# The order of the first loads of a pruned matrix product: a token pair ahead of the weights, on the other DMA queue

## The chip, the cores and the metric

The kernel runs on one core of one Trainium2 chip. The metric is the time of one execution on the device in microseconds (us), lower is better. The kernel before took 232.98 us (median of 3 runs, 232.91 to 233.33).

## The reference

A dense layer whose weight matrix is pruned on the fly. `x` is 16 x 512 x 1024 (8192 tokens of 1024 values), `w` is 1024 x 1024 and `b` has 1024 values, all in bf16. Down each column of `w` the rows form groups of four, and a weight is kept where its magnitude is at least the second largest of its group.

```python
wg = w.reshape(G, M, D)                       # G = 256, M = 4
mag = jnp.abs(wg)
order = jnp.argsort(mag, 1)
thr = jnp.take_along_axis(mag, order[:, M - N:M - N + 1, :], 1)   # N = 2
mask = mag >= thr
wp = (wg * mask).reshape(D, D)
return jnp.einsum("bsd,df->bsf", x, wp) + b
```

## The kernel before

The 8192 tokens are 64 tiles of 128. The product of a tile needs the tokens transposed (the 1024 input values on the partitions, in 8 blocks of 128) and the pruned weights. Two output halves `h` of 512 columns each fill one PSUM bank per tile.

Most tiles (14 to 63) are plain: their tokens come in through transposing DMAs, and 16 matmuls of 512 columns, one behind another, make a tile (L369); VectorE adds the bias and writes the output tile (L248). This part begins when all weights are pruned and takes about three quarters of the time.

Before that the weights have to be loaded and pruned, and TensorE should have work meanwhile. This is the front, whose order is written out by hand in the string `FRONT` (L285 to L299). One token of the string is one step, and each engine does its share of the steps in the string's order:

- `W` and `w`: a matmul on constants, 512 and 128 columns wide, whose result nobody reads (`warm`, L105). They fill TensorE's time at the start.
- `T.t`: tile t's first 512 input values are transposed by TensorE in four matmuls against an identity (L182); it waits for the tile's load. `C.t`: ScalarE copies them from PSUM (L187).
- `A.i` and `P.i`: VectorE takes the magnitudes of weight piece i (L120), then per group of four rows: `hi`, the larger of rows 0, 1 and of rows 2, 3 (L133); `lo`, the smaller of each (L134); `t1`, the smaller of the two `hi` (L137); `t2`, the larger of the two `lo` (L141); `thr`, the larger of `t1` and `t2` (L143); then the mask (L150) and the pruned weights (L153), for rows 0 and 1 first and rows 2 and 3 after them. On partition p of the weight tile lie the four rows of one group, so rows 0, 1 and rows 2, 3 are two halves of each partition. The threshold needs both halves.
- `N.i.t.m`: the matmuls of weight piece i with tile t for the rows m alone (L203); `M.i.t` is all four rows. Piece 0 is columns 0 to 255 of the first 512 input rows (its matmuls have 256 columns).

Piece 0 is the first that is needed. It comes in as two transfers of 128 KB, rows 0, 1 and rows 2, 3 (`load_w`, L71). Tokens 0 to 7 (their first 512 values) come in pairs or singly (`load_x`, L79): tiles 0 and 1 in one transfer of 256 KB, 2 and 3 in one, 4 and 5 singly with 128 KB each, 6 and 7 in one. Two DMA queues are used, that of the sync engine SP and that of ScalarE (ACT). Each queue does its transfers in order. ScalarE issues its transfers before it loads its function table and makes its first copy (L100).

The order of the first loads, by queue:

| queue | 1st | 2nd | 3rd | 4th | 5th | 6th |
|---|---|---|---|---|---|---|
| SP | piece 0 rows 0, 1 | tiles 0, 1 | tile 4 | tile 5 | piece 1 | tiles 6, 7 |
| ACT | piece 0 rows 2, 3 | tiles 2, 3 | | | | |

Then come larger transfers on SP: the second column half of the first 512 weight rows, another weight piece, and from L259 the transposed tokens of tiles 8 to 13.

Of the kernel before, what the change touches and what calls it, by code (L numbers as in the profile page):

```python
# [10 lines left out]
def kernel(  # L11
# [7 lines left out]
    nc = tc.nc  # L19
    P = 128  # L20
    bf16 = mybir.dt.bfloat16
    fp32 = mybir.dt.float32
    u16 = mybir.dt.uint16
    Alu = mybir.AluOpType
    Act = mybir.ActivationFunctionType
    K = tc.keep_in_program_order

    B, S, D = x.shape
# [10 lines left out]
    T, F = 8, 6  # L39
# [25 lines left out]
    def w_of(i):  # L65
        g, c0, c1 = pieces[i]
        return w_gh[(g, c0 // FH)][:, :, c0 % FH:c0 % FH + c1 - c0]

    def load_w(g, c0, c1, eng=nc.sync, m0=0, m1=4):
        dst = w_gh[(g, c0 // FH)][:, m0:m1, c0 % FH:c0 % FH + c1 - c0]  # L70
        K(eng.dma_start(dst, wv[:, g, m0:m1, c0:c1]))  # L71
# [4 lines left out]
    def load_x(ta, tb, eng=nc.sync):  # L76
        xt = const.tile([P, tb - ta, KH], bf16, name=f"xh_{ta}")
        src = xf[ta * P:tb * P, 0:KH].rearrange("(t p) c -> p t c", p=P)
        K(eng.dma_start(xt[:], src))  # L79
        for t in range(ta, tb):  # L80
            xh[t] = xt[:, t - ta, :]

    load_w(0, 0, 256, nc.sync, 0, 2)
    load_w(0, 0, 256, nc.scalar, 2, 4)
    load_x(0, 2)
    load_x(2, 4, nc.scalar)
    load_x(4, 5)
    load_x(5, 6)
    load_w(0, 256, 512)
    load_x(6, 8)  # L90
    load_w(0, 512, 1024)
# [14 lines left out]

    mags = {}

    def abs_piece(i, on_act):
        g, c0, c1 = pieces[i]  # L110
        n = c1 - c0
        if n <= 256:
            mag = mags_pool.tile([P, 4, n], bf16, name="mag")[:]
        else:
            mag = mag2_pool.tile([P, 4, n], bf16, name="mag2")[:]
        if on_act:
            K(nc.scalar.activation(mag, w_of(i), Act.Abs))
        else:
            for ms in (slice(0, 2), slice(2, 4)) if i == 0 else (slice(0, 4),):
                K(nc.vector.tensor_single_scalar(  # L120
                    mag[:, ms].bitcast(u16), w_of(i)[:, ms].bitcast(u16), 0x7FFF, op=Alu.bitwise_and))
        mags[i] = mag

    def prep_piece(i):
        g, c0, c1 = pieces[i]
        n = c1 - c0
        mag = mags.pop(i)
        magv = mag.rearrange("p (a j) f -> p a j f", j=2)
        hi = tmp.tile([P, 2, FH], bf16, name="hi")[:, :, :n]
        lo = tmp.tile([P, 2, FH], bf16, name="lo")[:, :, :n]  # L130
        for a in ((0, 1), (1, 2)) if i == 0 else ((0, 2),):
            a = slice(*a)
            K(nc.vector.tensor_tensor(hi[:, a], magv[:, a, 0, :], magv[:, a, 1, :], op=Alu.max))  # L133
        K(nc.vector.tensor_tensor(lo, magv[:, :, 0, :], magv[:, :, 1, :], op=Alu.min))  # L134
        t1 = tmp.tile([P, FH], bf16, name="t1")[:, :n]
        t2 = tmp.tile([P, FH], bf16, name="t2")[:, :n]
        K(nc.vector.tensor_tensor(t1, hi[:, 0, :], hi[:, 1, :], op=Alu.min))  # L137
        thr = tmp.tile([P, FH], bf16, name="thr")[:, :n]
        cols = (slice(0, n // 2), slice(n // 2, n)) if i == 0 else (slice(0, n),)
        for c in cols:  # L140
            K(nc.vector.tensor_tensor(t2[:, c], lo[:, 0, c], lo[:, 1, c], op=Alu.max))  # L141
        for c in cols:
            K(nc.vector.tensor_tensor(thr[:, c], t1[:, c], t2[:, c], op=Alu.max))  # L143
        mask = tmp.tile([P, 4, FH], bf16, name="mask")[:, :, :n]

        halves = (slice(0, 2), slice(2, 4)) if i < 3 else (slice(0, 4),)

        def keep(ms, c=slice(0, n)):
            tb = thr[:, None, c].to_broadcast([P, ms.stop - ms.start, c.stop - c.start])
            K(nc.vector.tensor_tensor(mask[:, ms, c], mag[:, ms, c], tb, op=Alu.is_ge))  # L150

        def prune(ms, c=slice(0, n)):
            K(nc.vector.tensor_tensor(w_of(i)[:, ms, c], w_of(i)[:, ms, c], mask[:, ms, c], op=Alu.mult))  # L153

        if i == 0:
            for step in (keep, prune):
                for c in cols:
                    step(halves[0], c)
            keep(halves[1])
            prune(halves[1])  # L160
        else:
            for ms in halves:
                keep(ms)
            for ms in halves:
                prune(ms)
# [100 lines left out]
    def issue_batch(t0, nb):  # L266
# [16 lines left out]


    FRONT = """  # L285
        I.1.0.512 D.0 A.0 P.0 W W W W W W W W W w w T.0 T.1 C.0 T.2 T.3 C.1 w T.4 C.2 N.0.0.0 N.0.0.1 T.5
        N.0.1.0 N.0.1.1 N.0.0.2 N.0.0.3 N.0.1.2 N.0.1.3 M.0.2 A.1 C.3 P.1 U.0.0.0.512 I.1.512.1024 G C.4 C.5
        M.0.3 N.0.4.0.1 T.6 T.7 C.6 N.0.4.2.3 C.7 A.2 M.0.5 M.0.6 P.2 M.0.7 N.1.0.0.1 N.1.1.0.1 A.3
        N.1.2.0.1 N.1.0.2.3 N.1.1.2.3 N.1.2.2.3 V.0.0 M.1.3 V.0.1 M.1.4 V.0.2 M.1.5 M.1.6 V.0.3 M.1.7 V.0.4
        P.3 N.2.0.0.1 V.0.5 N.2.1.0.1 N.2.0.2.3 V.0.6 N.2.1.2.3 M.2.2 V.0.7 M.2.3 M.2.4 M.2.5 M.2.6 A.4 P.4  # L290
# [9 lines left out]
    for tok in FRONT.split():  # L300
# [6 lines left out]
        elif k in "Ww":  # L307
            warm(FH if k == "W" else P)
        elif k == "A":
            abs_piece(n[0], n[0] == 3)  # L310
        elif k == "P":
            prep_piece(n[0])
        elif k == "T":
            transpose_half(n[0])
# [89 lines left out]
```

## Time and profile before

| what | value |
|---|---|
| median of three runs | 232.98 us |
| the profiled execution's own time | 232.85 us |
| its span, first to last instruction | 231.1 us |
| TensorE busy (matmul) | 226.7 us, 98% |
| VectorE busy | 120.2 us, 52% |
| ScalarE busy | 18.0 us, 8% |
| matmuls on constants (L105) | 12, 4.4 us busy |
| transposes on TensorE (L182) | 32 |
| matmuls of piece 0 and its like, 128x256 (L203) | 128 |

Times in the profile count from the start of the span. A matmul's busy time is its time in the pipeline, so matmuls overlap and the distance from one start to the next is their real pace. A group of several instructions in the timeline is given with its first start and its whole length.

### The profile page before, as it was taken

To read this page: it belongs to the slowest core of one execution; us is meant where nothing else is said; L and a number is where in the kernel's file an instruction comes from. 1 tells how busy PE (TensorE), PEld (TensorE's weight loads), DVE (VectorE), ACT (ScalarE), POOL (GpSimd) and SP (SyncE) were. 2 spreads that over 40 slices of the span, in tenths; PEclk is the share of its full clock that TensorE was granted. 3 is DMA by queue.
4 is the path that set the end of the run, shared out by engine and by line. 5 is a ranking of instruction groups with operands and counts; after the bars stand their busy time and mean duration, and the time that the engine had idled before them with its cause. 6 is when DMAs were issued, how large, how long until landed. Compare 5 with 4: busy or idle time off the path is not lost.

```text
span 231.1 us, 2772 instructions
## 1 busy us (share of the span) xinstructions
PE 226.7 (98%) x1137; PEld 111.1 (48%) x1156; DVE 120.2 (52%) x213; ACT 18.0 (8%) x33; POOL 0.7 (0%) x6
## 2 busy tenths in 40 slices
PE   8999999999999999999999999999999999999995
PEld 4887444444444444444444444444444444444443
DVE  4999787867987424424424424424423423433434
ACT  3868400000000000000000000000000000000000
POOL 1000000000000000000000000000000000000000
PEclk9999999999999999999999999999999999999999
DMA  6989989999447222991249522696128950122222
GB/s 214 299 180 262 210 195 197 289 247 318 185 182 272 91 84 80 272 249 59 80 115 278 152 95 91 129 245 194 70 91 197 241 197 34 60 91 91 91 94 91
DMA packets 77228, 38.19 MB, mean 165 GB/s; under 512 B 63136, under 2 KB 69024, under 8 KB 77216
## 3 DMA queue, kind: packets, MB, share of 16 engines
q1 hardware_dynamic: 67568, 20.88, 41.4%
q10 hardware_dynamic: 9648, 17.14, 20.1%
q8 instruction: 9, 0.15, 0.3%
q14 instruction: 3, 0.02, 0.0%
HBM read 3.41 MB, written 16.78 MB: 87 GB/s over the span
## 4 chain that ended last, share of the span: by engine, by line
PE 98%; DVE 0%; issue 0%
PE bank L369 73%; PE bank L203 16%; PE bank L263 6%; PE bank L105 2%; PE bank L182 1%; DVE o_last L354 0%
## 5 line engine op out<-in xcount | busy, mean ns | idle before, releaser
L369 PE MATMUL bank<-wp_nat,xTb 128*128 128x512 bf16 x737 | 161.7, 379 | 0.8
L248 DVE TENSOR_TENSOR o_pair<-bank,bias_sb 128x512 bf16<-128x512 f32 x104 | 67.3, 687 | 99.5 <-PE bank L369 94.1
L369 PEld LDWEIGHTS <-xTb 128*128 128x128 bf16 x752 | 73.6, 98 | 88.7
L239 DVE TENSOR_TENSOR stage<-bank,stage 128x512 f32<-128x512 f32 x22 | 14.2, 687 | 4.3 <-PE bank L203 4.2
L203 PE MATMUL bank<-w,xT 128*128 128x256 bf16 x128 | 14.5, 273 | 0.0
L243 DVE TENSOR_TENSOR o_pair<-stage,bias_sb 128x512 bf16<-128x512 f32 x22 | 14.0, 684 | 0.0
L203 PE MATMUL bank<-wp_nat,xg 128*128 128x512 bf16 x62 | 13.9, 379 | 0.1
L203 PEld LDWEIGHTS <-xT 128*128 128x128 bf16 x128 | 12.3, 98 | 1.6
L235 ACT COPY stage<-bank 128x512 f32<-128x512 f32 x22 | 11.5, 613 | 4.5 <-PE bank L203 4.5
L203 PE MATMUL bank<-wp_nat,xfill 128*128 128x512 bf16 x47 | 10.6, 379 | 0.1
L263 PE MATMUL bank<-wp_nat,xfill 128*128 128x512 bf16 x47 | 10.5, 379 | 0.1
L203 PEld LDWEIGHTS <-xg 128*128 128x128 bf16 x64 | 6.3, 98 | 7.6
L263 PEld LDWEIGHTS <-xfill 128*128 128x128 bf16 x48 | 4.7, 98 | 5.7
L203 PEld LDWEIGHTS <-xfill 128*128 128x128 bf16 x48 | 4.7, 98 | 5.5
L369 PE MATMUL bank<-wp_nat,xTs 128*128 128x512 bf16 x32 | 7.1, 379 | 0.0
L150 DVE TENSOR_TENSOR mask<-mag,thr 128x512 bf16<-128x512 bf16 (+3 forms) x10 | 5.6, 584 | 0.2
L153 DVE TENSOR_TENSOR w<-w,mask 128x512 bf16<-128x512 bf16 (+3 forms) x10 | 5.6, 582 | 0.1
L105 PE MATMUL bank<-const-bfloat16-1.0 128*128 128x512 bf16 (+1 forms) x12 | 4.4, 540 | 0.8 <-PEq L388 0.8
L369 PEld LDWEIGHTS <-xTs 128*128 128x128 bf16 x32 | 3.1, 98 | 3.8
L187 ACT COPY xT<-bank 128x512 bf16<-128x512 bf16 x8 | 4.1, 605 | 2.7 <-PE bank L182 2.7
L120 DVE TENSOR_SCALAR mag<-w 128x512 uint16<-128x512 uint16 (+2 forms) x6 | 2.7, 466 | 2.5 <-DMA w<-in_w_dram 2.5
L263 PE MATMUL bank<-wp_nat,xTb 128*128 128x64 bf16 (+3 forms) x40 | 3.7, 251 | 0.0
(20 smaller groups left out, 27.1 us busy)
## 6 DMA issues: line engine op xcount, KB each, us to landing
out_dram<-o_pair ACTq DMA_DIRECT2D x25, 512.0 KB, 2.8
out_dram<-o_pair ACTq DMA_DIRECT2D x13, 256.0 KB, 2.1
wp_nat<-w SPq DMA_DIRECT2D x16, 128.0 KB, 2.9
w<-in_w_dram SPq DMA_DIRECT2D x3, 512.0 KB, 5.5
xh<-in_x_dram SPq DMA_DIRECT2D x2, 256.0 KB, 4.1
xh<-in_x_dram ACTq DMA_DIRECT2D x1, 256.0 KB, 3.8
xh<-in_x_dram SPq DMA_DIRECT2D x2, 128.0 KB, 3.6
w<-in_w_dram SPq DMA_DIRECT2D x1, 256.0 KB, 4.0
```

What stands on the lines that cost most here:

```text
L105: K(nc.tensor.matmul(bank[7][:, :n], lhsT=ones[:, :P], rhs=ones[:, :n], start=True, stop=True))
L120: K(nc.vector.tensor_single_scalar(mag[:, ms].bitcast(u16), w_of(i)[:, ms].bitcast(u16), 0x7FFF, op=Alu.bitwise_and))
L150: K(nc.vector.tensor_tensor(mask[:, ms, c], mag[:, ms, c], tb, op=Alu.is_ge))
L153: K(nc.vector.tensor_tensor(w_of(i)[:, ms, c], w_of(i)[:, ms, c], mask[:, ms, c], op=Alu.mult))
L187: K(nc.scalar.copy(xt[:], src))
L203: K(nc.tensor.matmul(dst, lhsT=lhs, rhs=rhs, start=c0 == 0 and m == 0, stop=c1 == FH and m == 3))
L235: K(nc.scalar.copy(stage[(h, t)][:], bank[own[(h, t)]][:]))
L239: K(nc.vector.tensor_tensor(st, bank[own[(2 + h, t)]][:], st, op=Alu.add))
L243: K(nc.vector.tensor_tensor(get_o(t)[:, f], stage.pop((h, t))[:], bias_sb[:, f], op=Alu.add))
L248: K(nc.vector.tensor_tensor(get_o(t)[:, f], bank[bk][:], bias_sb[:, f], op=Alu.add))
L263: K(nc.tensor.matmul(bank[bk][:, :c1 - c0], lhsT=xN[t][:, kt, :], rhs=wp_nat[h][:, kt, c0:c1], start=kt == 0, stop=kt == KT - 1))
L369: K(nc.tensor.matmul(bank[bks[h]][:], lhsT=xN[t][:, kt, :], rhs=wp_nat[h][:, kt, :], start=kt == 0, stop=kt == KT - 1))
```

## The change

Four things change. The first token pair (tiles 0 and 1) becomes SP's first transfer, and both halves of weight piece 0 go on ScalarE's queue, as its first and second transfer. Tiles 4 and 5 become SP's second and third; the pair of tiles 2 and 3 becomes ScalarE's third. In `FRONT` the transposes run in the order of tiles 0, 1, 4, 5, 2, 3, all ahead of the first matmul of piece 0; the transposes of tile 5 had been behind the first two. The matmuls on constants go from nine wide and three narrow ones to seven wide and seven narrow ones, three of which stand ahead of tile 0, three between tiles 1 and 4, and one between tiles 2 and 3. On VectorE piece 0's magnitudes, `hi` and `lo` are now made for rows 0, 1 and then for rows 2, 3; before, both magnitudes came first, then both `hi`, then `lo` in one operation over both.

| queue | 1st | 2nd | 3rd | 4th | 5th |
|---|---|---|---|---|---|
| SP | tiles 0, 1 | tile 4 | tile 5 | piece 1 | tiles 6, 7 |
| ACT | piece 0 rows 0, 1 | piece 0 rows 2, 3 | tiles 2, 3 | | |

```diff
-    load_w(0, 0, 256, nc.sync, 0, 2)
+    load_x(0, 2)
+    load_w(0, 0, 256, nc.scalar, 0, 2)
+    load_x(4, 5)
     load_w(0, 0, 256, nc.scalar, 2, 4)
-    load_x(0, 2)
+    load_x(5, 6)
     load_x(2, 4, nc.scalar)
-    load_x(4, 5)
-    load_x(5, 6)
     load_w(0, 256, 512)
...
+    def abs_rows(mag, i, ms):
+        K(nc.vector.tensor_single_scalar(
+            mag[:, ms].bitcast(u16), w_of(i)[:, ms].bitcast(u16), 0x7FFF, op=Alu.bitwise_and))
...
-        else:
-            for ms in (slice(0, 2), slice(2, 4)) if i == 0 else (slice(0, 4),):
-                K(nc.vector.tensor_single_scalar(
-                    mag[:, ms].bitcast(u16), w_of(i)[:, ms].bitcast(u16), 0x7FFF, op=Alu.bitwise_and))
+        elif i > 0:
+            abs_rows(mag, i, slice(0, 4))
...
-        for a in ((0, 1), (1, 2)) if i == 0 else ((0, 2),):
-            a = slice(*a)
+        for a in (0, 1) if i == 0 else (slice(0, 2),):
+            if i == 0:
+                abs_rows(mag, i, slice(2 * a, 2 * a + 2))
             K(nc.vector.tensor_tensor(hi[:, a], magv[:, a, 0, :], magv[:, a, 1, :], op=Alu.max))
-        K(nc.vector.tensor_tensor(lo, magv[:, :, 0, :], magv[:, :, 1, :], op=Alu.min))
+            K(nc.vector.tensor_tensor(lo[:, a], magv[:, a, 0, :], magv[:, a, 1, :], op=Alu.min))
...
     FRONT = """
-        I.1.0.512 D.0 A.0 P.0 W W W W W W W W W w w T.0 T.1 C.0 T.2 T.3 C.1 w T.4 C.2 N.0.0.0 N.0.0.1 T.5
-        N.0.1.0 N.0.1.1 N.0.0.2 N.0.0.3 N.0.1.2 N.0.1.3 M.0.2 A.1 C.3 P.1 U.0.0.0.512 I.1.512.1024 G C.4 C.5
+        I.1.0.512 D.0 A.0 P.0 W W W W W W W w w w T.0 C.0 T.1 C.1 w w w T.4 T.5 T.2 C.2 w T.3
+        N.0.0.0 N.0.0.1 N.0.1.0 N.0.1.1 N.0.0.2 N.0.0.3 N.0.1.2 N.0.1.3 M.0.2 A.1 C.3 P.1 U.0.0.0.512 I.1.512.1024 G C.4 C.5
```

The rest of the string is the same. The lines below the first edit move down by three to four.

## The prediction

> **What bounds the kernel now.** I read the chain of work that ended last, in order of time, first.
>
> ```profile
> 0.77 4.21 PE bank L105 x11
> 4.99 1.28 PE bank L182 x16
> 6.26 0.06 PE bank L105
> 6.32 0.22 PE bank L182 x4
> 6.54 0.22 PE bank L203 x2
> 6.76 0.22 PE bank L182 x4
> 6.99 1.75 PE bank L203 x16
> ```
>
> It is TensorE (PE) from 0.77 us on without a break (98% of the span), so the whole run moves by whatever the front gains or loses: from 7 us on there is no stall in which a delay could be lost. The columns are start, length and number; this view counts by ends, the timeline below by starts, about 0.2 us earlier. A gain can only come from less work ahead of the real matmuls, a loss from a wait that TensorE doesn't have now. Next I read VectorE (DVE) and TensorE in the timeline.
>
> ```profile
> 3.35 0.51 DVE L120 TENSOR_SCALAR mag<-w 128x512 uint16<-128x512 uint16 x2 [2.47 <-DMA w<-in_w_dram]
> 3.77 0.49 DVE L133 TENSOR_TENSOR hi<-mag 128x256 bf16<-128x256 bf16 x2
> 4.17 0.42 DVE L134 TENSOR_TENSOR lo<-mag 128x512 bf16<-128x512 bf16 x1
> 4.51 0.29 DVE L137 TENSOR_TENSOR t<-hi 128x256 bf16<-128x256 bf16 x1
> 5.66 0.49 DVE L153 TENSOR_TENSOR w<-w,mask 128x256 bf16<-128x256 bf16 x2
> 6.52 0.43 DVE L153 TENSOR_TENSOR w<-w,mask 128x512 bf16<-128x512 bf16 x1
> 6.38 0.38 PE L203 MATMUL bank<-w,xT 128*128 128x256 bf16 x2
> 6.82 1.91 PE L203 MATMUL bank<-w,xT 128*128 128x256 bf16 x16
> ```
>
> VectorE waits 2.47 us for the weights and then works without a break: rows 0, 1 are pruned at 6.15 (5.66 + 0.49), rows 2, 3 at 6.95 (6.52 + 0.43). The first matmul with rows 2, 3, N.0.0.2, is the third of the last group: 16 matmuls take the 1.75 us from 6.82 to the next transposes at 8.57, 0.109 us each, so it starts at 7.04. That is 0.09 us after the weights are ready. A signal needs about 0.05 us (estimate: the last transpose of tile 0 ends at about 5.41 and ScalarE's copy starts at 5.45), which leaves about 0.04 us of slack. So VectorE's chain, which hangs on the landing of the weights, is all but a second bound, and N.0.0.2 is the place to compare: by then TensorE has done the transposes of tiles 0 to 5 and four matmuls, in both orders. Last I read the loads, issue by issue (median us to landing at the end; issue times from the timeline).
>
> ```profile
> w<-in_w_dram ACTq DMA_DIRECT2D x1, 128.0 KB, 2.8
> w<-in_w_dram SPq DMA_DIRECT2D x1, 128.0 KB, 2.6
> xh<-in_x_dram ACTq DMA_DIRECT2D x1, 256.0 KB, 3.8
> xh<-in_x_dram SPq DMA_DIRECT2D x1, 256.0 KB, 3.4
> ```
>
> The two w lines are issued at 0.73 and land at 3.33 and 3.53; the two token pairs are issued at 1.25 and land at 5.05 (ACT) and 4.65 (SP). The DMA engines move 344 GB/s between 2.4 and 3.2 us and 348 GB/s between 3.2 and 4.7: they are full, so what is put ahead of a transfer delays it.
>
> **The change, part by part.**
>
> *Weight rows 2, 3 land later.* They were the first transfer of ACT's queue (landing 3.53); now they are its second, issued at about 1.25, behind rows 0, 1, and SP's queue puts the token pair (256 KB) and tile 4 (128 KB) beside them. Low bound: as quick as the first one was, 1.25 + 2.8 = 4.05. High bound: as slow as the token pair that stands in that very place now, twice its size, 5.05. Value by bytes: 256 KB had landed by 3.53 and 768 KB (both halves and both pairs) by 5.05, 337 KB per us. Ahead of or beside the second half are 256 + 128 + 128 and its own 128 KB, 640 KB: 3.53 + 384/337 = 4.67; without tile 4, 4.29. I take 4.6, nearer the first, since tile 4 is issued in the same half microsecond.
>
> [...]
>
> *VectorE.* After the landing come 0.02 us to start (3.33 to 3.35), magnitudes 0.21 ((3.77 - 3.35)/2), `hi` 0.20 ((4.17 - 3.77)/2) and the half `lo` 0.20 (as a `hi` of its size; the whole one takes 4.51 - 4.17 = 0.34): 0.63 us to `t1`. The same three operations on rows 0, 1 lie under the wait, the extra 0.06 us of the split too; they end 0.63 us after that half lands, in time if it lands by 3.97 (a first ACT transfer lands at 3.53 now). So `t1` starts at 4.6 + 0.63 = 5.23 in place of 4.51: +0.72 us (bounds 4.05 and 5.05: +0.17 and +1.17). From `t1` on nothing changes, and rows 2, 3 are pruned at 7.67. Break-even without the slack is a landing at 3.88.
>
> *TensorE.* A wide constant matmul takes 0.427 us at the start (weight loads at 1.16, 1.58, 2.01), a 128-column one a quarter, 0.107; at 5.67 the pace doubles (16 matmuls of 256 columns in 1.75 us). Two wide ones fewer and four narrow ones more are four narrow units less. Laid out: seven wide to 3.76, three narrow to 4.08, T.0 and T.1 to 4.94, three narrow to 5.26, T.4 to 5.69, then at 0.055 each T.5 to 5.91, T.2 to 6.13, one narrow and T.3 to 6.41, four matmuls to 6.85. So TensorE alone reaches N.0.0.2 0.19 us sooner. It now waits there and ahead of N.0.0.0, 0.87 us in all (7.72 - 6.85), and the gain is swallowed. The transposes hide under this: tiles 0, 1 land by 4.13 at worst (0.73 + 3.4), tile 4 at about 4.29 (512 KB by the rate above), tile 5 by 5.42 (1.75 + 3.7). Tiles 2, 3, third on ACT, come with 1024 KB at 5.81, against 5.91 when T.2 is due; at the slowest landing of any of these loads (4.7) at 1.76 + 4.7 = 6.46, which gives N.0.0.2 at 6.46 + 0.98 = 7.44 (0.05 signal, 0.50 for T.2, w, T.3, 0.44 for four matmuls), still under 7.72. With the weights early, that would cost 0.40 us.
>
> *ScalarE* issues three transfers, not two: 0.5 us more (0.52 for the second), so its table load runs from 2.3 to 3.6 and its first copy ends at about 3.8; its first real copy is due at 4.75 (T.0's end 4.51 plus pipeline and signal), 0.95 us of cover. *SP* issues one transfer fewer before the big ones; these start about half a microsecond earlier, behind the small ones in the same queue, and TensorE needs them after 10 us. Nothing is gained or lost.
>
> *Sum.* +0.72 less the slack of 0.04 is +0.68 us. The profiled execution took 232.85 (span 231.1 and 1.75 around it, which the change does not touch), so 233.53; it lies 0.13 under the median of the three, so against the median 233.66.
>
> **The rivals.**
>
> 1. *The engines share by packets, not by bytes.* Weight packets hold 512 bytes, token packets 1024 (between 2.4 and 3.2 ACT's queue had 267 packets for 0.13 MB; later 272 for 0.26 MB). One for one, the weights get a third of 345 GB/s, 115, while SP has tokens. From 2.4 us, with 146 of SP's packets gone (about 0.12 MB), its other 390 KB last 1.7 us, to 4.1; 195 KB of weights are then through, and the other 61 KB at half rate take 0.35: 4.45, landing about 0.4 later (w rows 2, 3: packets to 3.1, landing 3.53): 4.85. Then +0.97 - 0.04 = 0.93 us: 233.91. For it: 214 and 267 packets of the two queues between 2.4 and 3.2; against: one queue often held fewer packets than the other, so the rows cannot tell.
>
> [...]
>
> 2. *ACT's queue is served sooner than the count says* (landing 4.05 to 4.35), or tiles 2, 3 become the gate: +0.13 to +0.43 us, 233.1 to 233.4. For it: ACT's first half started late (5 packets by 2.4 us) and still landed 0.2 us behind SP's.
>
> 3. *Not slower*: both halves land by about 3.7, so that pruning ends at 6.8 and TensorE's shorter filler decides: -0.19, 232.79. It decides below a landing of 3.88, which asks for 256 KB of weights in 1.1 us from 2.4 with some 0.14 MB of tiles 0, 1 left beside them. The rows speak against it.
>
> 4. *The pace doubles later.* Now it does so 4.9 us after the first matmul, over unbroken work. With two wide matmuls fewer and a wait of 0.87 us this could fail once and need another 4.9 us, to 10.6: from 7.7 the work runs at half pace, (10.6 - 7.7)/2 = 1.45 us on top, 235.1. The point is whether the pace is still slow at N.0.0.2. Against it: by my layout TensorE has no gap until 6.41.
>
> [...]
>
> **How the numbers follow.** Forecast 0.44, rival 1 0.20, rival 2 0.18, rival 3 0.11, rival 4 0.07. A measurement here can tell about 0.2%, 0.47 us, from no change: slower is above 233.45. Forecast and rival 1 lie above, but 0.02 of them may fall short; with rival 4 that is 0.69. Rivals 2 and 3 are the same, less 0.04 for a gain over 0.47 us, which no row gives: 0.27. The range goes from rival 3 to the high bound (1.17 - 0.04 = 1.13, 234.11): 232.8 to 234.15, leaving out rival 4 and the large gain. The likeliest case alone spans 233.3 to 234.1.
>
> **What would show it.** Right: in the changed kernel VectorE's second magnitude operation waits for a DMA until about 4.6, `t1` starts near 5.2, rows 2, 3 are pruned near 7.7, and TensorE has a gap ahead of N.0.0.0, the first it has. Rival 1: 4.85 and 5.5. Rival 3: no gap, N.0.0.2 at 6.85. Rival 4: matmuls of 256 columns 0.213 us apart after 8 us. I am wrong if the second half lands before 4.0, or if a stall behind 9 us appears or disappears.

## The result and the profile after

The changed kernel takes 234.30 us (median of 6 runs, 234.25 to 234.38). The kernel before took 233.16 in the same comparison (6 runs, 232.81 to 233.45). The ratio is 1.005, with a 95% interval of 1.0037 to 1.0063: 1.14 us slower. The two profiled executions took 234.32 and 232.85 us, 1.47 us apart; the one of before lies at the fast side of its own scatter.

First the chain of work that ended last in the changed kernel, in order of time (start, length, what).

```profile
0.74 3.73 DMA w<-in_w_dram
4.47 0.02 issue
4.49 0.30 DVE mag L110
...
5.11 0.20 DVE lo L137
5.32 0.23 DVE mag L110
...
7.99 0.44 DVE w L156
8.42 0.04 issue
8.47 1.69 PE bank L206 x14
```

Before, this chain was TensorE from 0.77 us on. Now it begins with a load of weights, goes through VectorE's whole pruning of piece 0, and reaches TensorE at 8.47, the start of N.0.0.2 (7.04 before). The load is that of rows 0, 1: it is issued at 0.74, and the chain goes straight from the `lo` of these rows into the second magnitude operation, that of rows 2, 3, with no DMA between them. Behind 8.47 it is TensorE without a gap, as before. So nearly all of the loss, 1.43 of the 1.47 us, lies ahead of it.

VectorE in the timeline of the changed kernel (start, length, engine, line, operation; in brackets the wait before it and what ended it):

```profile
4.49 0.29 DVE L110 TENSOR_SCALAR mag<-w 128x512 uint16<-128x512 uint16 x1 [3.62 <-DMA w<-in_w_dram]
4.82 0.29 DVE L136 TENSOR_TENSOR hi<-mag 128x256 bf16<-128x256 bf16 x1
5.03 0.29 DVE L137 TENSOR_TENSOR lo<-mag 128x256 bf16<-128x256 bf16 x1
5.24 0.29 DVE L110 TENSOR_SCALAR mag<-w 128x512 uint16<-128x512 uint16 x1
5.57 0.29 DVE L136 TENSOR_TENSOR hi<-mag 128x256 bf16<-128x256 bf16 x1
5.78 0.28 DVE L137 TENSOR_TENSOR lo<-mag 128x256 bf16<-128x256 bf16 x1
5.98 0.28 DVE L140 TENSOR_TENSOR t<-hi 128x256 bf16<-128x256 bf16 x1
...
7.99 0.43 DVE L156 TENSOR_TENSOR w<-w,mask 128x512 bf16<-128x512 bf16 x1
```

It waits 3.62 us, not 2.47, and it waits for rows 0, 1: the first transfer of ScalarE's queue landed at 3.53 before (rows 2, 3 then) and lands at 4.47 now. From 4.49 on VectorE works without a break. Its second magnitude operation starts at 5.24, 0.21 us after the `lo` of rows 0, 1, the same distance as from `hi` to `lo`, which wait for nothing from each other. Rows 2, 3, issued at 1.26, took 4.0 us, so they landed at about 5.2, just in time for it. So both halves are late, and in this kernel they bind at almost the same moment: 4.49 and 0.75 us of work on the first half give 5.24, and so does the landing of the second. `t1` starts at 5.98, where it had started at 4.51. From one magnitude operation to the `hi` that reads it are 0.33 us.

TensorE now has gaps, which it had nowhere before:

```profile
4.33 1.04 PE L185 MATMUL bank<-ident,xh 128*128 128x128 bf16 x8
...
6.58 0.41 PE L185 MATMUL bank<-ident,xh 128*128 128x128 bf16 x4 [0.34 <-DMA xh<-in_x_dram]
...
7.67 0.60 PE L206 MATMUL bank<-w,xT 128*128 128x256 bf16 x4 [0.39 <-ACT xT L190]
8.47 0.71 PE L206 MATMUL bank<-w,xT 128*128 128x256 bf16 x5 [0.20 <-DVE w L156]
```

It waits for tiles 2 and 3 until 6.58 (third on ScalarE's queue, 1.78 + 4.8), then ahead of the first matmul of piece 0 at 7.67. The view puts that one down to ScalarE's copy; the pruning of rows 0, 1 ends at 7.13 + 0.48 = 7.61, just ahead of it, so it is VectorE. The last wait is for rows 2, 3.

Last, the DMA engines in one stretch of 0.6 us. The columns are start and end, length, then busy us and instructions of PE, PEld (TensorE's weight loads), DVE, ACT and POOL; the last three are the granted clock of TensorE, the mean share of the 16 DMA engines and GB/s. The kernel before:

```profile
2.40:3.00 0.60, 0.60 (x3) 0.28 (x2) 0.00 (x0) 0.60 (x1) 0.00 (x0) 1.00 1.16 347
```

The changed kernel:

```profile
2.40:3.00 0.60, 0.60 (x3) 0.29 (x2) 0.00 (x0) 0.60 (x1) 0.00 (x0) 1.00 0.54 166
```

With the tokens first, the DMA engines move half as much in this stretch. I had taken them to be full from 2.4 us on.

### The profile page after: what moved, and what is told of

Its sections match the earlier page's. It is cut to its first block, busy times and chain, and to the rows that moved or that the text cites. A ratio compares the mean times of both kernels' runs of the same rounds, so it can differ in the third digit from the quotient of the medians.

```text
span 232.5 us, 2796 instructions
## 1 busy us (share of the span) xinstructions
PE 228.1 (98%) x1158; PEld 111.4 (48%) x1158; DVE 120.5 (52%) x214; ACT 18.1 (8%) x33; POOL 0.7 (0%) x6
## 3 DMA queue, kind: packets, MB, share of 16 engines
HBM read 3.41 MB, written 16.78 MB: 87 GB/s over the span
## 4 chain that ended last, share of the span: by engine, by line
PE 95%; DVE 2%; DMA 2%; issue 0%
PE bank L372 73%; PE bank L206 16%; PE bank L266 6%; DMA w<-in_w_dram 2%; DVE o_last L357 0%; DVE w L156 0%; DVE mask L153 0%; DVE hi L136 0%; DVE mag L110 0%; PE bank L185 0%; DVE lo L137 0%; DVE thr L146 0%; DVE t L144 0%; DVE t L140 0%
```

## The experiments

Three questions: which part of the change costs the time, why rows 2, 3 land so late, and what the shorter filling of TensorE does. Each diff is against the kernel before or the changed kernel, as said; the median of the kernel before was 233.02 to 233.06 in these comparisons.

### Which part costs the time

**loads_only**: the kernel before with the new order of the loads.

```diff
-    load_w(0, 0, 256, nc.sync, 0, 2)
+    load_x(0, 2)
+    load_w(0, 0, 256, nc.scalar, 0, 2)
+    load_x(4, 5)
     load_w(0, 0, 256, nc.scalar, 2, 4)
-    load_x(0, 2)
+    load_x(5, 6)
     load_x(2, 4, nc.scalar)
-    load_x(4, 5)
-    load_x(5, 6)
```

> The kernel before with the new order of the loads alone (old string, old order on VectorE). Theory (the landing of weight rows 2, 3 sets the time): they land near 5.2 us as in the changed kernel, VectorE then still has one magnitude operation, both hi and the whole lo to do, 0.95 us, so t1 starts near 6.2, rows 2, 3 are pruned near 8.6 and N.0.0.2 starts near 8.7, against 7.04 before and 8.47 after: +1.6 us, about 234.8. Rival (the tokens of tiles 2 and 3, third on ScalarE's queue, are the gate through TensorE's order): tile 2 starts near 6.55, the first matmul of piece 0 near 7.3, N.0.0.2 near 7.95: +0.9 us, about 234.1.

Measured: 234.49 us, ratio 1.0065 (1.0052 to 1.0078), 1.47 us over the kernel before. VectorE in its timeline:

```profile
5.22 0.29 DVE L120 TENSOR_SCALAR mag<-w 128x512 uint16<-128x512 uint16 x1 [0.51 <-DMA w<-in_w_dram]
5.43 0.48 DVE L133 TENSOR_TENSOR hi<-mag 128x256 bf16<-128x256 bf16 x2
5.83 0.42 DVE L134 TENSOR_TENSOR lo<-mag 128x512 bf16<-128x512 bf16 x1
6.17 0.28 DVE L137 TENSOR_TENSOR t<-hi 128x256 bf16<-128x256 bf16 x1
...
8.17 0.43 DVE L153 TENSOR_TENSOR w<-w,mask 128x512 bf16<-128x512 bf16 x1
```

In the old order VectorE has nothing to do between the two magnitude operations: it waits 0.51 us for rows 2, 3, which land at 5.2, and has pruned them at 8.60. So the theory's steps came; its time, 234.8, was 0.3 us too high. The order of the loads alone makes the kernel as slow as the whole change does, a little slower even. The rival's 234.1 through the late tiles is excluded.

**front_only**: the kernel before with the new string.

```diff
-        ... W W W W W W W W W w w T.0 T.1 C.0 T.2 T.3 C.1 w T.4 C.2 N.0.0.0 N.0.0.1 T.5
+        ... W W W W W W W w w w T.0 C.0 T.1 C.1 w w w T.4 T.5 T.2 C.2 w T.3 N.0.0.0 N.0.0.1
```

> The kernel before with the new string alone (old loads, old order on VectorE). Theory: the string costs nothing, because pruning ends at 6.95 as before and N.0.0.2 starts at 7.0 to 7.05: within 0.2 us of the kernel before, about 233.2. Rival (fewer matmuls on constants and a gap ahead of tile 0, which lands at 4.67, make the clock come up a step later): the pace doubles after 8 us and the time rises by 0.5 us or more.

Measured: 233.30 us, ratio 1.0028 (1.0008 to 1.0048), but scattered from 232.97 to 235.2 over 12 runs. The median is 0.28 us above the kernel before, more than the theory's 0.2, and its reason does not hold in the profiled execution (233.38 us): pruning ends there at 6.97, but TensorE waits 0.79 us for tile 0 and 0.42 us for tile 4, and N.0.0.2 starts only at about 7.52. So with the old loads the string does cost something; with the new ones this is hidden behind the pruning (no_split below has the new string and takes 234.47, loads_only the old one and takes 234.49). Four of the twelve runs (233.60, 234.44, 235.19, 235.20) are as long as the rival has it. The section on the clock below comes back to them.

**split_only**: the kernel before with the new order on VectorE.

```diff
...
-        for a in ((0, 1), (1, 2)) if i == 0 else ((0, 2),):
-            a = slice(*a)
+        for a in (0, 1) if i == 0 else (slice(0, 2),):
+            if i == 0:
+                abs_rows(mag, i, slice(2 * a, 2 * a + 2))
             K(nc.vector.tensor_tensor(hi[:, a], magv[:, a, 0, :], magv[:, a, 1, :], op=Alu.max))
-        K(nc.vector.tensor_tensor(lo, magv[:, :, 0, :], magv[:, :, 1, :], op=Alu.min))
+            K(nc.vector.tensor_tensor(lo[:, a], magv[:, a, 0, :], magv[:, a, 1, :], op=Alu.min))
```

> The kernel before with the new order on VectorE alone (old loads, old string). Theory (an operation that needs the result of the one just before it starts 0.33 us after it, one with another in between 0.21): magnitudes at 3.35, hi at 3.67, lo at 3.88, magnitudes of rows 2, 3 at 4.08, hi at 4.41, lo at 4.62, t1 at 4.82 in place of 4.51, rows 2, 3 pruned at 7.26, N.0.0.2 at 7.31: +0.27 us, about 233.45. Rival (as I predicted, only the 0.06 us of the split lo counts): +0.02 us, about 233.2.

Measured: 233.12 us, ratio 1.0004 (0.9996 to 1.0013). In its profile `t1` starts at 4.80 and rows 2, 3 are pruned at 7.23 (4.51 and 6.95 before), as the theory has it, and against the profiled execution of before, 232.85, the time is up by the 0.27 us foreseen. Against the median it is 0.10, which can't be told from nothing: the theory's 233.45 did not come, and the rival's 233.2 is nearer. The kernel before may lose some 0.2 us elsewhere in its longer runs; only a short one was profiled, so this is not shown.

**no_split**: the changed kernel with the old order on VectorE, the reverse of that edit.

> The changed kernel with the old order on VectorE (new loads, new string). Theory: rows 2, 3 land near 5.2 and N.0.0.2 starts near 8.7, so +1.6 us against the kernel before, about 234.8, 0.2 us more than the changed kernel; the new order on VectorE pays where the second half lands late. Rival (tiles 2 and 3 are the gate): the same 234.3 as the changed kernel.

Measured: 234.47 us, ratio 1.0068 (1.0055 to 1.008); 234.30 with the new order. Rows 2, 3 are pruned at 8.61, 0.19 us later than in the changed kernel. So the difference that the theory named came, though its 234.8 did not. By the end of pruning, the new order on VectorE costs 0.28 us with the old loads (7.23 against 6.95) and gives back 0.19 with the new ones, where the first half can be worked on under the wait.

Over all kernels one rule comes out. The table sets the end of pruning of rows 2, 3 in each profile beside the time of the same profiled execution.

| kernel | second magnitude operation starts | rows 2, 3 pruned | execution | difference |
|---|---|---|---|---|
| before | 3.56 | 6.95 | 232.85 | 225.90 |
| split_only | 4.07 | 7.23 | 233.12 | 225.89 |
| tok_512 | 4.80 | 7.97 | 233.95 | 225.98 |
| tok_act | 5.00 | 8.38 | 234.24 | 225.86 |
| changed | 5.24 | 8.42 | 234.32 | 225.90 |
| loads_only | 5.22 | 8.60 | 234.48 | 225.88 |
| no_split | 5.23 | 8.61 | 234.47 | 225.86 |
| x4_first | 5.83 | 8.99 | 234.88 | 225.89 |

Over two microseconds the time follows the end of pruning; the difference stays within 0.12 us. Pruning ends 3.38 to 3.39 us after the second magnitude operation starts in the old order on VectorE, and 3.16 to 3.18 in the new one. That start is the landing of rows 2, 3 where VectorE waits for it (tok_act, loads_only, no_split, x4_first). In the changed kernel and tok_512 it comes straight behind the work on rows 0, 1, which landed at 4.47 and 4.02. The other five kernels are bound by TensorE, by its work or by its waits for tokens, and lie above the rule: w1k_first at 226.01, front_9w and front_only at 226.4, w_second at 228.5, singles at 229.0.

### Why rows 2, 3 land late

They landed at 5.2, and I had expected 4.6; rows 0, 1 landed at 4.47, and I had counted on 3.53. Five kernels change what comes first.

**tok_512**: the changed kernel, its first token pair as two transfers of 128 KB with rows of 512 bytes.

```diff
-    load_x(0, 2)
+    load_x(0, 2, cuts=(0, KH // 2, KH))
...
-        K(eng.dma_start(xt[:], src))
+        for c0, c1 in zip(cuts, cuts[1:]):
+            K(eng.dma_start(xt[:, :, c0:c1], src[:, :, c0:c1]))
```

> The changed kernel with the first token pair as two transfers of 128 KB with rows of 512 bytes, the size and form of the weight halves. Theory (reading the tokens starts slowly): 2.4 to 3.0 us still under 220 GB/s and rows 2, 3 land at 4.9 to 5.3; time 234.0 to 234.4. Rival (packets of 1024 bytes are at fault): over 300 GB/s from 2.4 to 3.0, landing near 4.5, time near 233.6.

Measured: 233.94 us, ratio 1.0039 (1.0024 to 1.0054). From 2.4 to 3.0 us the engines move 273 GB/s (and only 61 from 1.8 to 2.4), so neither side's number came; the second magnitude operation starts at 4.80, 0.44 us sooner than in the changed kernel, again straight behind the work on rows 0, 1, which landed 0.45 us sooner (4.02). Rows of 512 bytes on both queues let the weights through sooner.

**x4_first**: the changed kernel with tile 4 ahead of the pair on SP.

```diff
-    load_x(0, 2)
+    load_x(4, 5)
     load_w(0, 0, 256, nc.scalar, 0, 2)
-    load_x(4, 5)
+    load_x(0, 2)
```

> The changed kernel with tile 4 (128 KB, one tile) as SP's first transfer and the pair of tiles 0, 1 as its second. Theory (any token tile first starts slowly): under 220 GB/s from 2.4 to 3.0, rows 2, 3 land near 5.2, N.0.0.2 as in the changed kernel, time near 234.3 though tiles 0, 1 land later. Rival (the transfer of two tiles is at fault): over 300 GB/s, rows 2, 3 land near 4.7, time near 233.8.

Measured: 234.66 us, ratio 1.0068 (1.0044 to 1.0091), scattered from 233.96 to 235.19. 293 GB/s from 2.4 to 3.0, so a single tile first does not start slowly; the first weight half is there at 3.60. Yet VectorE gets the second only at 5.83; the pair is beside it now. The theory's reason fell, and the rival's landing at 4.7 too.

**tok_act**: the kernel before with both weight halves on SP and the pair first on ScalarE's queue.

```diff
     load_w(0, 0, 256, nc.sync, 0, 2)
-    load_w(0, 0, 256, nc.scalar, 2, 4)
-    load_x(0, 2)
+    load_x(0, 2, nc.scalar)
+    load_w(0, 0, 256, nc.sync, 2, 4)
     load_x(2, 4, nc.scalar)
```

> The kernel before with both weight halves first and second on SP's queue and the pair of tiles 0, 1 first on ScalarE's, so weights are the first transfer of all. Theory (the engines start slowly only where tokens are SP's first transfer): between 2.4 and 3.0 us they move over 300 GB/s as before; rows 2, 3, now second in their queue and beside the tokens, land near 4.4; with 0.97 us from there to t1, N.0.0.2 starts near 7.9 and the time is near 233.9. Rival (tokens early in either queue slow the start): under 220 GB/s from 2.4 to 3.0, rows 2, 3 land after 4.8, time 234.2 or more.

Measured: 234.21 us, ratio 1.0048 (1.0031 to 1.0065); 209 GB/s from 2.4 to 3.0; second half at 5.00. The rival holds: the pair early in either queue slows the start (166 GB/s with it first on SP in the changed kernel, 347 in the kernel before), and it does not help that weights are the first transfer of all.

**w1k_first**: the kernel before, SP's first transfer 256 KB of w in rows of 1024 bytes.

```diff
-    load_w(0, 0, 256, nc.sync, 0, 2)
+    load_w(0, 0, 512, nc.sync, 0, 2)
...
-    load_w(0, 256, 512)
+    load_w(0, 256, 512, nc.sync, 2, 4)
```

> The kernel before, with rows 0, 1 of weight pieces 0 and 1 as SP's first transfer, so that it has the token pair's size and packets (256 KB in rows of 1024 bytes) but reads w; piece 1 then loads rows 2, 3 alone. Theory (it is reading the tokens that starts slowly): 2.4 to 3.0 us at over 300 GB/s, rows 0, 1 land near 3.7, the time is 0.2 to 0.5 us above the kernel before. Rival (large packets or a large first transfer start slowly): under 220 GB/s from 2.4 to 3.0, both halves land after 4.0, time 233.8 or more.

Measured: 233.46 us, ratio 1.0018 (1.0009 to 1.0028); 197 GB/s from 1.8 to 2.4 and 262 from 2.4 to 3.0, so less than the theory's 300 in that stretch but more in the one before (129 in the kernel before). Rows 0, 1 are at hand at 3.75 and rows 2, 3 by 3.96. So this transfer of 256 KB in rows of 1024 bytes, which reads w, does not start slowly. What the time loses is a wait of TensorE for tiles 0 and 1 (0.63 us, until 5.62).

**w_second**: the changed kernel with weight piece 1 first on SP and the pair second.

```diff
-    load_x(0, 2)
+    load_w(0, 256, 512)
     load_w(0, 0, 256, nc.scalar, 0, 2)
-    load_x(4, 5)
+    load_x(0, 2)
     load_w(0, 0, 256, nc.scalar, 2, 4)
-    load_x(5, 6)
+    load_x(4, 5)
     load_x(2, 4, nc.scalar)
-    load_w(0, 256, 512)
+    load_x(5, 6)
```

> The changed kernel, except that SP's first transfer is weight piece 1 (256 KB of w in rows of 512 bytes) and the pair of tiles 0, 1 its second: both halves of piece 0 keep their place on ScalarE's queue, the same number of bytes is ahead on SP, but no tokens come first. Theory (part of the lateness is a slow start on the tokens): 2.4 to 3.0 us at over 300 GB/s, rows 2, 3 land near 4.5, and N.0.0.2, 3.25 us behind the landing as in the changed kernel (5.22 to 8.47), starts near 7.8 unless the later tiles hold it up to 8.0: time 233.8 to 234.0. Rival (the place on ScalarE's queue alone makes it late): landing at 5.0 or later, N.0.0.2 at 8.25 or later, 234.2 or more.

Measured: 235.85 us, ratio 1.0098 (1.0063 to 1.0133), 234.19 to 236.31. The landing came as the theory had it: the second magnitude operation starts at 4.48 and rows 2, 3 are pruned at 7.65. The place on ScalarE's queue alone explains no landing at 5.2. The time did not follow: tiles 0 and 1 now came so late that TensorE waited 2.18 us for them, and in the profiled execution (236.13) its clock fell afterwards, which the next section shows. The fastest run, 234.19, is not far from the theory's 234.0. In this kernel ScalarE's queue also got its packets first (226 against 9 from 1.8 to 2.4 us), so part of its quick landing may be that.

How the two queues share is seen in the changed kernel itself, between 3.1 and 3.5 us, when SP moves tokens and ScalarE's queue weights (packets, MB, share of 16 engines):

```profile
q1 hardware_dynamic: 82, 0.08, 58.6%
q10 hardware_dynamic: 91, 0.04, 37.6%
```

About as many packets from each, and half the bytes for the one with the small rows. In the kernel before, where both move tokens in rows of 1024 bytes from 3.2 to 4.7 us, it is 274 and 272 packets, and 0.26 MB each. So in these two stretches, where both queues had work, they shared by packets. Counts over 0.4 and 1.5 us don't show whether single rows took turns, and not every stretch has equal counts: from 2.4 to 3.0 us the changed kernel has 73 packets of tokens and 48 of weights.

### The filling of TensorE and the clock

**front_9w**: front_only with nine wide and two narrow matmuls on constants ahead of tile 0 and one ahead of tile 4.

```diff
-        ... W W W W W W W w w w T.0 C.0 T.1 C.1 w w w T.4
+        ... W W W W W W W W W w w T.0 C.0 T.1 C.1 w T.4
```

> The kernel before with the new string, but with nine wide and two narrow matmuls on constants ahead of tile 0 and one ahead of tile 4, as before. Theory (the scatter of front_only, 232.97 to 235.2, is the clock, which comes up late in some runs when TensorE has a gap of 0.6 to 0.8 us ahead of tile 0): the scatter goes, highest under 233.7, median within 0.3 us of the kernel before. Rival (the scatter comes from the order of the transposes and their late tiles): runs over 234 remain.

Measured: 233.22 us, ratio 1.0005 (0.9996 to 1.0013), 233.02 to 233.49 over 11 runs. The scatter is gone with the gap. (front_only stood idle for 0.79 us ahead of tile 0 in its profile; here there is no wait.) That the clock is what made the longest runs of front_only long is not shown, since none of them was profiled. w_second shows a fall of the clock behind a longer gap (2.18 us). Windows of its profile, with the columns as above:

```profile
4.48:7.89 3.41, 1.47 (x23) 1.33 (x24) 3.34 (x15) 1.02 (x2) 0.00 (x0) 1.00 1.05 355
7.89:11.30 3.41, 3.41 (x23) 2.62 (x21) 3.31 (x11) 2.15 (x5) 0.00 (x0) 0.50 1.16 299
11.30:14.00 2.70, 2.70 (x30) 2.32 (x29) 2.59 (x10) 1.76 (x3) 0.00 (x0) 1.00 1.14 240
```

The clock was half from 7.89 to 11.30, for 3.41 us. In the 3.41 us before that, a stretch that I chose by this length, TensorE was busy for 1.47 us, and 20 of its 23 matmuls there are transposes. The longest time without a matmul before the fall was 2.18 us. Whether that wait or the low share of busy time brought the fall, this profile does not tell.

**singles**: a try to beat both, the kernel before with tiles 0 and 1 loaded one on each queue and one wide matmul on constants less.

```diff
-    load_x(0, 2)
+    load_x(0, 1)
+    load_x(1, 2, nc.scalar)
     load_x(2, 4, nc.scalar)
...
-        ... W W W W W W W W W w w T.0 T.1
+        ... W W W W W W W W w w T.0 T.1
```

> The kernel before with tiles 0 and 1 loaded singly, one on each queue, right behind the weight halves, and one wide matmul on constants fewer: a try to beat both. Theory (the kernel before is bound by two things at once, weights at 7.0 us and TensorE's work behind tile 0, which lands at 4.67): tile 0 lands near 4.3, TensorE is 0.3 us ahead, N.0.0.2 waits for the pruning at 7.0 in every run: 232.7 to 232.85 with less scatter. Rival (the extra issue delays the tiles behind, or the clock comes up late): 233.0 or more.

Measured: 236.18 us, ratio 1.0132 (1.0118 to 1.0146). Rows 2, 3 were pruned at 6.94, but tiles 2 and 3, now third on ScalarE's queue, took 5.5 us to land, and TensorE waited for them:

```profile
4.35 1.06 PE L183 MATMUL bank<-ident,xh 128*128 128x128 bf16 x8
7.39 1.04 PE L183 MATMUL bank<-ident,xh 128*128 128x128 bf16 x8 [1.98 <-DMA xh<-in_x_dram]
...
8.76 0.63 PE L204 MATMUL bank<-w,xT 128*128 128x256 bf16 x2
```

A gap of 2 us, and two matmuls of 256 columns take 0.43 us (8.76 to 9.19), double their time in the kernel before (16 in 1.75 us). No kernel tried here beats the one before.

## Why the prediction was right and wrong

The direction was right, and so was the place (N.0.0.2 waits for the pruning); the size was too small: +0.68 us foreseen, +1.14 between the medians and +1.47 between the profiled executions. 234.30 lies above the range, whose top was 234.15. N.0.0.2 started at 8.47 and not at 7.72, and these 0.75 us come from two steps, the landing of the weights (0.62) and VectorE's work behind it (0.13). By its steps:

- *Weight rows 2, 3 land later*: the mechanism was right, and the order of the loads alone carries the loss (loads_only). The size is the step that failed: 4.6 was taken, 4.05 to 5.05 allowed, and they land at 5.2. Two things were missing. First, the count by bytes is wrong, as the queues shared by packets where both had work (82 against 91 from 3.1 to 3.5 us); rival 1, worked out from that, gave 4.85. Second, the DMA engines were not full from 2.4 us on. From 1.8 to 2.4 the changed kernel moves 87 GB/s in place of 129 and from 2.4 to 3.0 166 in place of 347, (42 + 181) x 0.6 = 134 KB less, which at some 345 GB/s is 0.39 us (estimate). 4.85 and 0.39 make 5.24; this sum was made afterwards, no run separates its two terms, and that it comes so close is in part luck. (Rival 1 took 0.12 MB of tokens to be through by 2.4 us; 51 packets, 0.05 MB, were.) The high bound was none: the pair that stands in this place before had weights ahead of it, no tokens.
- *Rows 0, 1 under the wait*: this step failed as well. The prediction let VectorE do the first half while it waits for the second, "in time if it lands by 3.97 (a first ACT transfer lands at 3.53 now)". That left out the token pair beside it on SP: rows 0, 1 landed at 4.47, and the second magnitude operation could start only at 5.24. So even with rows 2, 3 at 4.6 nothing would have been gained, and the sign that was named, that this second operation waits for a DMA, is not there; the first one waits. Either half alone gives 5.2.
- *VectorE*: from the start of that magnitude operation to `t1` 0.61 us was foreseen (0.63 from the landing), and it is 0.74 (5.24 to 5.98). I had taken the distance from one operation to the next from a row where another stands between an operation and the one that reads its result, 0.21 us; directly behind one another it is 0.33. From `t1` on nothing changed (2.44 us to the end of pruning in both).
- *TensorE*: filler that is taken away gains nothing, as foreseen; the layout to 6.85 did not happen, since tiles 0, 1 came at 4.3 and not by 4.13, and tiles 2, 3 at 6.5, later even than the worst case of 6.46. Both hide under the pruning, as the prediction said that they would. (Tile 5's 1.75 + 3.7 there is 5.45, not 5.42; nothing hangs on it.)
- *ScalarE and SP*: right. ScalarE's first copy ends at 3.80 (3.60 + 0.20), as worked out, and nothing behind 9 us changed.
- *Rival 1* is the nearest, and the forecast, rival 1 and the high end all lay on the same side of the truth. *Rival 3* needed the weights by 3.88. *Rival 4* did not happen in the changed kernel, whose runs lie within 0.13 us of one another. Whether it is what makes some runs of the same string with the old loads long is not shown; in singles, behind a gap of 2 us, the pace is still slow at 9 us.

The base adds to the miss: the kernel before is near 232.85 in some runs and up to 233.5 in others, so a sum against its fastest executions and a ratio of medians differ by 0.2 to 0.3 us.

## What to carry to other kernels

Where two transfers share the DMA engines, count packets and not bytes: here the one with rows of 512 bytes moved 0.04 MB with 91 packets while the one with rows of 1024 moved 0.08 MB with 82, and something large put beside it on another queue delayed it too. The first transfer of ScalarE's queue, with nothing ahead of it, landed 0.94 us later (4.47 against 3.53) once a token pair stood beside it. Check each transfer that a chain needs, not only the last. Price a moved load from a row that has the same things ahead of it; the same place in the queue behind other data is no bound. Before taking out matmuls on constants that look like waste, see whether a gap arises where they stood: front_only, with a wait of 0.79 us there, scattered up to 235.2 us, and front_9w, with none, up to 233.49. That the clock links the two is not shown.

## What was not expected of the hardware

- With the token pair as first transfer the DMA engines run half empty until 3.0 us (166 GB/s in place of 347 in the changed kernel, 166 and 165 in loads_only and no_split); with w first in rows of the same size, or one token tile first, they do not (262 and 293). Counted from 1.8 to 3.0 us, 152 KB move in the changed kernel, 286 in the kernel before, 275 in w1k_first, 271 in x4_first, and about 200 in tok_512 and tok_act. Why reading the pair starts slowly is open: these runs tell that it is neither the row size alone nor the queue; what it is they do not tell.
- One VectorE operation behind the one whose result it reads starts 0.33 us after it, with an independent one in between 0.21 (tiles of 256 to 512 values per partition).
- In w_second TensorE's clock fell to half (0.50) for 3.41 us; the longest time without a matmul before it was 2.18 us, and in the 3.41 us ahead of the fall TensorE was busy for 1.47.
- The clock column does not show every slow stretch: in singles it reads 1.00 from 8.1 to 10 us, while two matmuls of 256 columns take 0.43 us there (8.76 to 9.19), twice the time of the kernel before (16 in 1.75 us).
